# Weights' first matrix requested in another order beside the q and k of two attention groups, and one cast moved to ScalarE

## Chip, core and metric

The kernel runs on one core of one Trainium2 chip. The metric is the device time of one execution in microseconds (us); the median of seven executions is used. A profiled execution gives the trace from which all other times here are read, counted from the start of its span.

## What is computed

Causal attention in blocks of 64 over 8 batches, 8 heads, 576 positions and a head size of 64, followed by a two-branch layer over the 4608 tokens. Cut to what matters:

```python
scores = q @ k.T / 8                      # per batch and head, 576 x 576
scores = where(block_i >= block_j, scores, -1e9)
attn   = softmax(scores)
x      = (attn @ v), heads side by side   # 4608 x 512
h1, h2 = x @ w1, x @ w2                   # w1, w2: 512 x 1024
out    = maximum(h1, h2) @ w_out          # 1024 x 512
```

The kernel uses max(h1, h2) = h2 + max(h1 - h2, 0). So it needs D = w1 - w2 (`d_sb`, in bf16), M = w2 @ w_out (`m_sb`), and then out = x @ M + relu(x @ D) @ w_out.

## The kernel before, in words

**Work and tiles.** The 64 heads form 32 pairs, two pairs are a group, two groups a batch. For a group, `load_qk` fetches q and k as fp32 (0.59 MB each, issued by SP, after POOL has written one element of the target tile, which makes the request wait its turn: "gated"). `cast` makes bf16 of them, `transposes` turns them on TensorE into PSUM tiles that DVE or ScalarE copy to `qT` and `kT`. Scores (L376, and L394 with padded keys `kz`) go to PSUM, ScalarE takes exp of them into `aT` (L400), POOL zeroes the masked corners (L405), `av` multiplies with v (L491) and DVE normalises (L497, L498). `x_out` or a transposing DMA puts the result into `xT`. v is fetched by POOL in five chunks for a batch (`load_v(b, c)`), cast to bf16 on the way; the last chunk has 64 rows.

**The layer's work is filler.** `plan` lists units in a fixed order: `bT_unit` (transposes of w2), `m_unit(i, c)` (eight matmuls, one quarter of a half of M; the result is copied from PSUM to `m_sb` at L254), `h_unit(i, f)` (four matmuls with columns f of D; DVE's relu at L231 makes `g`), `y_unit`. `fill(n)` at places in the code issues the next units of the list worth n. Block j of `d_sb` (256 columns, made by `diff_w(j)` on DVE at L183 from `w1raw` and w2) is used by `h_unit(i, 2j)` and `h_unit(i, 2j + 1)`.

**The order is written out by hand.** The scheduler is off: each engine runs its instructions in the order in which the code issues them, and waits where one needs something that is not there. There are queues of this kind on PE, DVE, ScalarE (ACT), POOL and SP. POOL's queue holds casts, masks and the issue of the loads of v, w1, w2 and w_out (L159, L177, L180, L189); SP's holds the loads of q and k (L115) and the stores. Up to group 3 the order is in straight code (from L584), later a loop from L691 does one group per turn.

**Buffers.** `ps_m` has four PSUM buffers that m_units, h_units, transposes and av take in turn, so a matmul waits until the buffer's last user has been copied out. q and k have three fp32 buffers each, w1 has four, one for a block.

**The stretch at hand.** The filler ahead of group 2's q transposes is m(0,3), m(1,0) and m(1,1); m(1,2) follows q's transposes, m(1,3) k's; then come the first scores of pair 4, h_unit(0,0) and h_unit(0,1), the rest of pair 4's scores, h(0,2) and h(0,3), group 3's q transposes, h(0,4), group 3's k transposes, h(0,5), and with pair 6 the loop, whose first `av` is that of pair 4 with batch 1's v.

Of the kernel before, what the change touches and what calls it, by code (L numbers as in the profile page):

```python
# [14 lines left out]
def kernel(  # L15
# [18 lines left out]
    d_ff = moe_w1.shape[1]  # L34
# [9 lines left out]
    RPP = S // NP  # L44
# [53 lines left out]
    m_sb = wpool.tile([P, NDM, d_model], BF16, name="m_sb")  # L98
# [6 lines left out]
    dve, pool, act = nc.vector.tensor_copy, nc.gpsimd.tensor_copy, nc.scalar.copy  # L105

    def load_qk(g, queues, gated=False):
        b, u = divmod(g, GPB)
        for nm, src, queue in (("q", q, queues[0]), ("k", k, queues[1])):
            if queue is None or by_dma(nm, g):  # L110
                continue
            raws[nm, g] = t = raw.tile([P, 2, RPP * D], FP32, name=f"{nm}raw")
            if gated:
                nc.gpsimd.memset(t[:, 0, :1], 0.0)
            queue.dma_start(  # L115
                out=t[:],
                in_=src[b, 4 * u:4 * u + 4].rearrange(
                    "(s h) (p t) d -> (h p) s (t d)", h=2, t=RPP),
            )
# [4 lines left out]
    def by_dma(nm, g):  # L124
        return g >= T_DMA.get(nm, NG)
# [21 lines left out]
    def cast(nm, g, parts):  # L147
        if by_dma(nm, g):
            return
        t = raws[nm, g].rearrange("p s (t d) -> p t s d", d=D)  # L150
        if (nm, g) not in qk_n:
            qk_n[nm, g] = qkn.tile([P, RPP, 2, D], BF16, name=f"{nm}n")
        n = qk_n[nm, g]
        for copy, j0, j1 in parts:
            copy(out=n[:, j0:j1], in_=t[:, j0:j1])  # L155

    def load_v(b, c):
        rows = min(P, S - c * P)
        nc.gpsimd.dma_start(  # L159
            out=vv_r[b % NV][P - rows:, c, :, :D],  # L160
            in_=v[b, :, c * P:c * P + rows, :].rearrange("h p d -> p h d"),
        )
# [5 lines left out]
    WB = 256  # L168
# [6 lines left out]
    def load_w1(j):  # L175
        w1_raw[j] = wraw.tile([P, NDM, WB], FP32, name="w1raw")
        nc.gpsimd.dma_start(out=w1_raw[j][:], in_=w1r[:, :, j * WB:(j + 1) * WB])  # L177
# [4 lines left out]
    def diff_w(j):  # L182
        nc.vector.tensor_sub(d_sb[:, :, j * WB:(j + 1) * WB], w1_raw[j][:], w2_sb[j])  # L183
# [8 lines left out]
    dve, pool, act = nc.vector.tensor_copy, nc.gpsimd.tensor_copy, nc.scalar.copy  # L192
    SP, ACT = nc.sync, nc.scalar
# [51 lines left out]
    def m_unit(i, c):  # L245
        ds = slice(i * WH, (i + 1) * WH)
        pt = ps_m.tile([P, WH], FP32, name="ps_M", tag="m")
        for f in range(NFF):
            nc.tensor.matmul(  # L249
                pt[:], bT_sb[:, f, c * P:(c + 1) * P], wo_sb[:, f, ds],  # L250
                start=(f == 0), stop=(f == NFF - 1),
            )
            if f == NFF - 1:
                (act if i else dve)(out=m_sb[:, c, ds], in_=pt[:])  # L254
            yield

    def y_terms(i, s):
# [69 lines left out]
    def fill(n):  # L327
        while n > 0:
            if not current:
                k = next((k for k, t in enumerate(todo) if t[2] <= done_tokens[0]), None)  # L330
                if k is None:
                    return max(0, n)
                current.append(todo.pop(k))
            t = current[0]
            next(t[1])
            n -= t[3]
            t[0] -= 1
            if not t[0]:
                current.pop()
        return 0  # L340
# [10 lines left out]
    def transposes(nm, g, copies):  # L351
        n = qk_n.pop((nm, g))
        pts = [ps_m.tile([P, RPP, NP], BF16, name=f"ps_{nm}T", tag="m") for _ in range(2)]
        for j in range(RPP):
            for i in range(2):
                r = slice(i * NP, (i + 1) * NP)
                nc.tensor.transpose(  # L357
                    pts[i][:, j, :], n[r, j].rearrange("p s d -> p (s d)"), ident[r, r],
                )

        def copy_out(which=(0, 1), part=(0, NP), copy=None):
            p0, p1 = part
            for i in which:
                t = (qT_r if nm == "q" else kT_r)[(2 * g + i) % NT]
                (copy or copies[i])(  # L365
                    out=t[:, p0 * RPP:p1 * RPP].rearrange("q (p j) -> q p j", j=RPP),
                    in_=pts[i][:, :, p0:p1].rearrange("q j p -> q p j"),
                )
        return copy_out

    def scores(p, ps, col, c, q0, w):
        qT, kT = qT_r[p % NT], kT_r[p % NT]
        k0 = min(c * P, S - P)
        for hh in range(2):
            r = slice(hh * D, (hh + 1) * D)
            nc.tensor.matmul(  # L376
                ps[:, hh, col:col + w], kT[r, k0:k0 + P], qT[r, q0:q0 + w],
                start=True, stop=True,
            )


    def pad_keys(p):
        nc.gpsimd.tensor_copy(
            out=kz_r[p % NT].rearrange("p (a c) -> p a c", c=BLK)[:, 0:3:2],
            in_=kT_r[p % NT][:, S - 3 * BLK:].rearrange("p (a c) -> p a c", c=BLK)[:, 0:3:2],
        )


    def corner_scores(p, ps, col):
        qT, kz = qT_r[p % NT], kz_r[p % NT]  # L390
        for k0, q0 in ((0, 384), (BLK, 512)):
            for hh in range(2):
                r = slice(hh * D, (hh + 1) * D)
                nc.tensor.matmul(  # L394
                    ps[:, hh, col:col + BLK], kz[r, k0:k0 + P], qT[r, q0:q0 + BLK],
                    start=(k0 == 0), stop=(k0 > 0),
                )

    def exp(p, ps, w, a0):
        nc.scalar.activation(  # L400
            out=aT_r[p % NA][:, :, a0:a0 + w], in_=ps[:, :, :w], func=AF.Exp, scale=scale,
        )

    def mask(p, a0, eng=None):
        (eng or nc.gpsimd).memset(aT_r[p % NA][BLK:, :, a0:a0 + BLK], 0.0)  # L405
# [23 lines left out]
    def masks_p(p, eng=None):  # L429
        for a in (0, 256):  # L430
            mask(p, a, eng)

    def masks_q(p, eng=None):
        for a in (1024, 1408):
            mask(p, a, eng)
# [3 lines left out]
    def tile_0(p):  # L439
        u = ps_s.tile([P, 2, 512], FP32, name="ps_s", tag="s")  # L440
        scores(p, u, 0, 0, 0, 512)
        return lambda masked: (exp(p, u, 512, 0), masked and mask(p, 0))

    def tile_1(p):
        u = ps_s.tile([P, 2, 512], FP32, name="ps_s", tag="s")
        scores(p, u, 0, 0, 512, 64)
        scores(p, u, 64, 1, 128, 448)
        return lambda masked: (exp(p, u, 512, 512), masked and mask(p, 576))

    def tile_2(p):  # L450
        u = ps_s.tile([P, 2, 512], FP32, name="ps_s", tag="s")
        corner_scores(p, u, 320)
        scores(p, u, 0, 2, 256, 320)
        scores(p, u, 384, 3, 448, P)

        def out(masked):
            exp(p, u, 512, 1024)
            nc.scalar.activation(
                out=aT_r[p % NA][BLK:, :, 1536:AW], in_=u[BLK:, :, 320:320 + BLK],
                func=AF.Exp, scale=scale,  # L460
            )
            if masked:
                mask(p, 1024)
                mask(p, 1344)
        return out

    def masks(p):
        for a0 in (0, 576, 1024, 1344):
            mask(p, a0)

    def region(*tiles, masked=True):
        for out in tiles:
            out(masked)
# [146 lines left out]
    burst_p(3, 1)  # L620
    masks_p(2)
    masks_p(3)
    load_w1(0)
    fill(2)
    av(1, [2, 3, 4])
    burst_q1(2)
# [4 lines left out]
    burst_q3(2)  # L631
    masks_q(2)
    load_qk(2, (SP, SP), gated=True)
    load_w1(1)
    load_w1(2)
    fill(2)
    burst_q1(3)
    fill(2)
# [2 lines left out]
    av(2, [2, 3, 4])  # L641
    burst_q3(3)
    masks_q(3)
    load_w1(3)
    load_v(1, 0)
    load_v(1, 1)
    load_qk(3, (SP, SP), gated=True)
    fill(8)
    av(3, [2, 3, 4])
    fill(4)  # L650
    x_out(1, 0, NCH, (act, act))
    cast("q", 2, ((pool, 0, RPP),))
    cast("k", 2, ((pool, 0, RPP),))
    load_v(1, 2)
    fill(4)
    diff_w(0)
    diff_w(1)
    fill(8)
    transposes("q", 2, (dve, act))()
    diff_w(2)  # L660
    fill(4)
    transposes("k", 2, (act, act))()
    pad_keys(4)
    pad_keys(5)
    diff_w(3)
    cast("q", 3, ((pool, 0, RPP),))
    load_v(1, 3)
    load_qk(4, (SP, SP), gated=True)
    cast("k", 3, ((pool, 0, RPP),))
# [1 line left out]
    fill(4)  # L671
    region(tile_0(4), tile_1(4), masked=False)
    fill(8)
    region(tile_2(4), tile_0(5), masked=False)
    masks(4)
    fill(8)
    copy_out = transposes("q", 3, (dve, act))
    outs = tile_1(5), tile_2(5)
    copy_out()
# [96 lines left out]
```

## Time and profile before

| | us |
|---|---|
| median of 7 executions | 261.57 (261.13 to 262.75) |
| the profiled execution, its own time | 260.73 |
| its span, first to last instruction | 259.0 |
| PE busy | 242.6 |
| DVE, ACT, POOL busy | 149.1, 120.4, 122.9 |

The mean granted TensorE clock of the span was 0.993. Rows of a timeline give the start, the duration, the engine, the line and the operation. A group of waits reads "who, line, waited for <- whom: total, times, longest". A row of the table by time gives the stretch, its length, busy time of PE, PEld (weight loads), DVE, ACT and POOL with the number of instructions, and then PE's granted clock, the DMA engines' share and GB/s. A transfer's landing is counted from the start of its issue.

### The profile page before, as it was taken

The page shows a single profiled execution, that of the slowest core. Times are in us where ns is not written, and L with a number is a line of the kernel's source. Part 1 is how long each engine was busy: PE and PEld are TensorE (multiplying, and loading weights), DVE is VectorE, ACT ScalarE, POOL GpSimd, SP SyncE. Part 2 cuts the span into 40 slices and gives each one's busy share as a digit, 9 for nine tenths or more (in the row PEclk, how much of TensorE's full clock was granted, in tenths as well). Part 3 has the DMA queues.
Part 4 walks back from the last instruction along what each step waited for, and adds up shares of the span by engine and source line. Part 5 has one row for each costly group of instructions (what it writes and reads, how often), then busy time and mean ns, then how long its engine had stood idle before and what let it go on. Part 6 is the DMA issues. An engine that isn't in the chain of part 4 may idle for free.

```text
span 259.0 us, 6717 instructions
## 1 busy us (share of the span) xinstructions
PE 242.6 (94%) x2732; PEld 133.5 (52%) x2768; DVE 149.1 (58%) x299; ACT 120.4 (46%) x160; POOL 122.9 (47%) x289
## 2 busy tenths in 40 slices
PE   8798849999999999999999999999999999999994
PEld 2466734556464655555555555555555554444443
DVE  4977564756485537653764476447644754754521
ACT  2876237784956647373646464555555400000000
POOL 2976436549778684857494658456331100000000
PEclk9999988999999999999999999999999999999999
DMA  7999999469999999999999999999952302101122
GB/s 244 210 162 233 370 296 182 80 180 195 143 203 163 176 174 196 219 176 212 172 215 144 223 171 201 152 205 179 130 101 84 86 31 75 66 19 65 56 105 83
DMA packets 104383, 41.27 MB, mean 159 GB/s; under 512 B 89248, under 2 KB 93728, under 8 KB 104352
## 3 DMA queue, kind: packets, MB, share of 16 engines
q0 software_dynamic: 65952, 11.87, 59.5%
q1 hardware_dynamic: 37984, 28.32, 47.8%
q10 hardware_dynamic: 416, 0.66, 0.8%
q8 instruction: 21, 0.34, 0.6%
q14 instruction: 10, 0.08, 0.1%
HBM read 34.60 MB, written 9.44 MB: 170 GB/s over the span
## 4 chain that ended last, share of the span: by engine, by line
PE 88%; DMA 5%; ACT 2%; issue 2%; DVE 1%; POOL 1%; SPq 0%; POOLq 0%
PE ps_y L268 35%; PE ps_h L226 24%; PE ps_o L491 11%; PE ps_s L376 9%; DMA kraw<-in_k_dram 5%; PE ps_w L346 2%; PE ps_qT L357 2%; ACT aT L400 1%; PE ps_y L283 1%; PE ps_s L394 1%; PE ps_M L249 1%; PE ps_s L411 1%; PE ps_kT L357 1%; POOL kn L155 0%; PE ps_bT L238 0%
## 5 line engine op out<-in xcount | busy, mean ns | idle before, releaser
L400 ACT ACTIVATE aT<-ps_s 128x1024 bf16<-128x1024 f32 (+2 forms) x100 | 95.8, 994 | 44.4 <-PE ps_s L376 32.8
L268 PE MATMUL ps_y<-wo_sb,g 128*128 128x512 bf16 x261 | 66.7, 379 | 2.6 <-issue 2.5
L226 PE MATMUL ps_h<-xT,d_sb 128*128 128x512 bf16 x277 | 67.2, 380 | 1.2 <-issue 0.6
L231 DVE TENSOR_SCALAR g<-ps_h 128x512 bf16<-128x512 f32 x72 | 49.7, 690 | 21.3 <-PE ps_h L226 21.3
L405 POOL MEMSET aT<- 64x128 bf16 x128 | 22.9, 201 | 62.4 <-ACT aT L400 60.9
L273 DVE COPY y<-ps_y 128x512 f32<-128x512 f32 x35 | 24.2, 692 | 46.2 <-PE ps_y L268 45.6
L491 PEld LDWEIGHTS <-aT 128*128 128x128 bf16 x960 | 37.5, 98 | 14.1 <-issue 0.7
L226 PEld LDWEIGHTS <-d_sb 128*128 128x128 bf16 x288 | 26.4, 98 | 31.5 <-issue 3.6
L268 PEld LDWEIGHTS <-g 128*128 128x128 bf16 x280 | 24.7, 98 | 30.2 <-issue 5.5
L491 PE MATMUL ps_o<-vv,aT 128*128 128x65 bf16 x960 | 39.9, 194 | 0.0
L268 PE MATMUL ps_y<-m_sb,xT 128*128 128x512 bf16 x136 | 37.2, 379 | 0.4 <-PE ps_s L376 0.2
L159 POOL DMA_DIRECT2D vv<-in_v_dram x40 | 34.0, 854 | 0.9 <-issue 0.5
L376 PE MATMUL ps_s<-qT,kT 64*128 64x128 bf16 (+6 forms) x344 | 31.8, 283 | 1.4 <-ACT kT L365 0.7
L498 DVE TENSOR_TENSOR xp<-ps_o,rec 128x256 bf16<-128x256 f32 (+1 forms) x64 | 31.4, 491 | 2.2
L132 POOL DMA_DIRECT2D kb<-in_k_dram x40 | 29.4, 758 | 0.0
L497 DVE RECIPROCAL rec<-ps_o 128x4 f32<-128x4 f32 (+1 forms) x64 | 12.0, 187 | 24.2 <-PE ps_o L491 23.6
L288 ACT COPY y<-ps_y 128x256 f32<-128x256 f32 (+1 forms) x2 | 0.6, 320 | 49.3 <-PE ps_y L283 49.3
L365 ACT COPY qT<-ps_qT 128x576 bf16<-128x576 bf16 x15 | 9.6, 640 | 24.4 <-PE ps_qT L357 23.0
L155 POOL CAST qn<-qraw 128x1152 bf16<-128x1152 f32 (+1 forms) x15 | 17.0, 1135 | 7.9 <-DMA qraw<-in_q_dram 7.9
L268 PEld LDWEIGHTS <-xT 128*128 128x128 bf16 x140 | 12.8, 98 | 14.0 <-issue 0.7
L376 PEld LDWEIGHTS <-kT 64*128 64x128 bf16 x344 | 11.9, 95 | 12.6 <-issue 7.8
L365 DVE COPY qT<-ps_qT 128x576 bf16<-128x576 bf16 x17 | 12.7, 749 | 0.5 <-PE ps_qT L357 0.5
(58 smaller groups left out, 137.1 us busy)
## 6 DMA issues: line engine op xcount, KB each, us to landing
qraw<-in_q_dram SPq DMA_DIRECT2D x16, 576.0 KB, 5.2
out_dram<-y SPq DMA_DIRECT2D x35, 256.0 KB, 4.0
vv<-in_v_dram POOLq DMA_DIRECT2D x32, 128.0 KB, 5.9
kraw<-in_k_dram SPq DMA_DIRECT2D x5, 576.0 KB, 7.6
kb<-in_k_dram POOLq DMA_DIRECT2D x40, 72.0 KB, 6.8
w1raw<-in_moe_w_dram POOLq DMA_DIRECT2D x4, 512.0 KB, 11.5
xT<-in_moe_w_dram POOLq DMA_DIRECT2D x4, 256.0 KB, 6.9
wo_sb<-in_moe_w_out_dram POOLq DMA_DIRECT2D x2, 512.0 KB, 10.4
```

The lines of the kernel that those rows point to most:

```text
L132: nc.gpsimd.dma_start(out=n[h * BLK:(h + 1) * BLK, :, s], in_=(q if nm == "q" else k)[b, 4 * u + 2 * s + h].rearrange("(j p) d -> p j d", ...
L159: nc.gpsimd.dma_start(out=vv_r[b % NV][P - rows:, c, :, :D], in_=v[b, :, c * P:c * P + rows, :].rearrange("h p d -> p h d"),)
L226: nc.tensor.matmul(pt[:], d_sb[:, c, f * P:(f + 1) * P], xT[:, c, t0:t0 + SPAN], start=(c == 0), stop=(c == NDM - 1),)
L231: nc.vector.tensor_scalar_max(g[:, f], pt[:], 0.0)
L268: nc.tensor.matmul(py[:], lhs, rhs, start=(n == 0), stop=(n == len(terms) - 1),)
L273: nc.vector.tensor_copy(out=y[:], in_=py[:])
L365: (copy or copies[i])(out=t[:, p0 * RPP:p1 * RPP].rearrange("q (p j) -> q p j", j=RPP), in_=pts[i][:, :, p0:p1].rearrange("q j p -> q p j"),)
L376: nc.tensor.matmul(ps[:, hh, col:col + w], kT[r, k0:k0 + P], qT[r, q0:q0 + w], start=True, stop=True,)
L400: nc.scalar.activation(out=aT_r[p % NA][:, :, a0:a0 + w], in_=ps[:, :, :w], func=AF.Exp, scale=scale,)
L405: (eng or nc.gpsimd).memset(aT_r[p % NA][BLK:, :, a0:a0 + BLK], 0.0)
L491: nc.tensor.matmul(po[:, gi, hh, :], a[:, hh, a0:a0 + P], vv[:, c, h0 + 2 * hh, :], start=(mm == 0), stop=(mm == n_mm - 1),)
L498: nc.vector.tensor_mul(xp[:, :, ts[0]:ts[0] + n, p % 2].rearrange("q s t d -> q t s d"), po[:, :, :, :D], rec[:, :n].to_broadcast([P, n, 2 ...
```

## The change

It moves requests and steps in the hand-written order, from POOL's and DVE's queues above all. In words:

- `load_w1(0)` goes behind the masks of pair 3; `load_w1(1)` to `(3)` go behind the cast of group 2's q, which goes forward.
- Group 3's q is requested ahead of that cast, its k behind it.
- Batch 1's v chunks 0 and 1 follow the blocks of w1; chunk 2 is issued after the cast of group 3's q, beside chunk 3.
- Group 2's k is cast by ScalarE instead of POOL, behind `x_out(1)`.
- `diff_w(1)` to `(3)` move back, to behind k's transposes and between the h_units.
- The PSUM copies of m(1,0) and m(1,1) go from ScalarE to DVE.

```diff
-                (act if i else dve)(out=m_sb[:, c, ds], in_=pt[:])
+                (act if i and c > 1 else dve)(out=m_sb[:, c, ds], in_=pt[:])
...
     masks_p(3)
-    load_w1(0)
     fill(2)
...
     load_qk(2, (SP, SP), gated=True)
-    load_w1(1)
-    load_w1(2)
     fill(2)
...
     masks_q(3)
-    load_w1(3)
+    load_w1(0)
+    load_qk(3, (SP, None), gated=True)
+    cast("q", 2, ((pool, 0, RPP),))
+    load_qk(3, (None, SP), gated=True)
+    for j in range(1, d_ff // WB):
+        load_w1(j)
     load_v(1, 0)
     load_v(1, 1)
-    load_qk(3, (SP, SP), gated=True)
     fill(8)
     av(3, [2, 3, 4])
     fill(4)
     x_out(1, 0, NCH, (act, act))
-    cast("q", 2, ((pool, 0, RPP),))
-    cast("k", 2, ((pool, 0, RPP),))
-    load_v(1, 2)
+    cast("k", 2, ((act, 0, RPP),))
     fill(4)
     diff_w(0)
-    diff_w(1)
     fill(8)
     transposes("q", 2, (dve, act))()
-    diff_w(2)
     fill(4)
     transposes("k", 2, (act, act))()
     pad_keys(4)
     pad_keys(5)
-    diff_w(3)
+    diff_w(1)
     cast("q", 3, ((pool, 0, RPP),))
+    load_v(1, 2)
     load_v(1, 3)
     load_qk(4, (SP, SP), gated=True)
     cast("k", 3, ((pool, 0, RPP),))
...
     region(tile_0(4), tile_1(4), masked=False)
     fill(8)
+    diff_w(2)
     region(tile_2(4), tile_0(5), masked=False)
     masks(4)
     fill(8)
+    diff_w(3)
     copy_out = transposes("q", 3, (dve, act))
```

## Prediction

> **What bounds the kernel now.** I read the page first, then the chain of waits in order of time, then PE's waits, then the rows of the transfers, then the table by microsecond. Times without a unit are microseconds (us) from the span's start.
>
> ```profile
> PE 242.6 (94%) x2732; PEld 133.5 (52%) x2768; DVE 149.1 (58%) x299; ACT 120.4 (46%) x160; POOL 122.9 (47%) x289
> PE 88%; DMA 5%; ACT 2%; issue 2%; DVE 1%; POOL 1%; SPq 0%; POOLq 0%
> ```
>
> TensorE is busy 94% of the span and is 88% of the chain that ended last. Only one other thing has weight: DMA with 5%, and the chain in order of time shows that this is a single piece.
>
> ```profile
> 22.23 13.25 DMA kraw<-in_k_dram
> 35.60 1.16 POOL kn L155
> 36.81 0.47 PE ps_kT L357 x18
> 37.28 1.82 PE ps_M L249 x8
> 39.09 0.97 PE ps_s L376 x6
> 40.06 0.33 issue
> 40.39 1.73 PE ps_h L226 x7
> ```
>
> Group 2's k is asked for at 22.23 and lands 13.25 later; POOL casts it, and only then can PE transpose it. PE's own waits, and its clock just after, give the price:
>
> ```profile
> PE ps_kT L357 <- POOL kn L155: 3.3, 1, 3.3
> PE ps_qT L357 <- POOL qn L155: 1.0, 1, 1.0
> ...
> 37.00:38.00 1.00, 1.00 (x22) 0.70 (x15) 0.98 (x1) 0.69 (x2) 0.58 (x1) 0.54 1.91 217
> 38.00:39.00 1.00, 1.00 (x6) 0.45 (x3) 0.00 (x0) 0.48 (x1) 0.75 (x3) 0.50 1.70 136
> 39.00:40.00 1.00, 1.00 (x7) 0.30 (x7) 0.00 (x0) 0.62 (x2) 1.00 (x2) 0.50 1.65 105
> 40.00:41.00 1.00, 0.67 (x5) 0.47 (x5) 0.00 (x0) 1.00 (x2) 1.00 (x4) 0.75 0.39 31
> ```
>
> PE loses 3.3 for k and 1.0 for q. After the 3.3 its granted clock (third number from the end) is about a half until 40.5: eight matmuls of L249 take 1.82, where eight took 0.87 earlier; six of scores take 0.97 instead of 0.61. That is 1.4 more, so some 5.7 lie in this place. Everything behind it is PE work, back to back, so what is won here and not given back shows in the total.
>
> **Why k is late: the bytes in front of it.**
>
> ```profile
> L177 POOL DMA_DIRECT2D w1raw<-in_moe_w_dram x4: 751/754/767, 18.4 to 24.4; - x4
> DMA to landing us min/median/max: 10.1/11.5/12.3
> ...
> 23.00:24.00 1.00, 0.52 (x13) 0.30 (x9) 0.87 (x3) 1.00 (x2) 0.63 (x2) 1.00 1.46 194
> 24.00:25.00 1.00, 0.58 (x6) 0.53 (x7) 0.16 (x1) 0.05 (x1) 0.85 (x2) 1.00 1.40 264
> 25.00:26.00 1.00, 1.00 (x12) 0.90 (x10) 0.42 (x1) 0.00 (x0) 1.00 (x3) 1.00 1.10 381
> ```
>
> The last column is GB/s. Up to about 24.8 the small pieces of w_out hold it at 200; then it runs at 340 to 390 until 37. I take 0.36 MB/us. The blocks of w1 (0.52 MB each) land at 29.8, 32.0, 34.3 and 36.65; q and k of group 2 (0.59 MB each) at 30.2 and 35.5; of group 3 at 37.25 and 39.0. They take turns: 3.87 MB from 24.8 to q3 make 10.7, which is 35.6, so a landing comes some 1 to 1.6 after that sum.
>
> **The change, part by part.** *Moved requests.* SP still asks for q2 and k2 at 21.8 and 22.2. In front of k2 now lie only q2 and w1's block 0 (issued by POOL at 24.35, behind two memsets): 1.70 MB, 4.7, so 29.5 and with the lag 30.7 (35.5 before). For q2, with its own bytes and some of block 0, 27.7 and the lag: 29.2. For block 0 the nearest rows give two ends: one block in turns takes 2.3 (the distance of the landings) after w_out's last landing at 27.5, so 29.8; behind all that is asked for earlier (q2, k2, q3: 2.29 MB in all) 31.2 to 31.6. I take 30.6, the middle. *DMA: Bandwidth & Descriptors* of the Trainium skill, section "Anatomy of one DMA", gives a transfer 2.0 us plus bytes over 436 GB/s: 3.2 for a block, which would land at 27.6 and cost PE nothing. The rows say 10.1 to 12.3 for a block in company, so I stay with the bytes in front; by the page the sum below would be 0.8 better at its first step.
>
> *PE up to the first h_unit.* m(1,1) ends at 31.09 as before. q's cast (1.15, on POOL) ends at 30.4, or 30.9 if it meets DVE's subtraction as before (it took 1.65 then): q's wait of 1.0 is gone, transposes to 31.5. New is that DVE has diff_w(0) in front of the PSUM copies of m(1,0) and m(1,1), which ScalarE did: 30.6 + 1.23 + 0.42 = 32.3 before m(1,2) gets its buffer. That is a new PE wait of 0.8. m(1,2) to 33.15. k's cast on ScalarE: 640 elements took 0.725 at the start, 1152 by ScalarE's about 1.04 ns each 1.27; 30.7 + 1.27 = 32.0, and q's copy queued behind it (0.64) ends at 32.65, under m(1,2). k's transposes 33.15 to 33.5, m(1,3) to 34.4 with kT's copy under it, scores to 35.0. So h_unit(0,0) starts at 35.0 instead of 40.39: 5.4 won.
>
> *DVE behind it.* The subtractions now stand between the relus and, the last, in front of qT's copy of group 3. Block 1 is issued at about 30.5 and shares with k3: (0.52 + 0.59)/0.36 from 32.2 is 35.3. diff_w(1) ends near 36.7. Then DVE has until group 3's k copy, which the scores of pair 6 need: five relus of 0.69, two subtractions of 1.23, two copies of 0.75: 7.4, less 0.6 since DVE's rows start about 0.07 before the one ahead has ended: 43.5. Those scores began at 47.85, so of 5.4 there are 4.2 left. Blocks 2 and 3 (1.05 MB more: 38.2) are there in time.
>
> *POOL's queue.* POOL now waits for q2 with q3's memset behind it done, but with k3's memset (it gates SP's request), three blocks of w1 (0.75 each), v(1,0) and v(1,1) (0.89 each), the key pads, q3's cast, v(1,2), v(1,3), q4 and k4's memsets, k3's cast and v(1,4) queued. From 30.4 that gives: k3 30.5, blocks to 32.8, v(1,1) 34.6, q3's cast 36.7, v(1,3) 38.4, q4 38.5, v(1,4) to 40.4. SP's order is the same, its waits are for those memsets. k3 and q4 are asked for 3.0 later and 2.4 earlier than before, v(1,0) 7.7 later, v(1,4) 1.6 earlier.
>
> *What is late next.* av of pair 4 needs v(1,4). Before, it was issued at 41.9, landed 7.1 later at 49.0 and was used at 50.69. The bytes after 24.8 are the same as before. After: 2.29 MB to 31.2, a hole to 32.2 until k3 and block 1 arrive, k3 and three blocks 2.16 MB to 38.2, four v of 0.131 MB at 0.105 MB/us (the row 39 to 40, where v ran alone) 5.0, q4 and k4 3.3, v(1,4) 0.6: 47.1, landing about 47.4; with q2 a microsecond later, and a hole as long as that of before (31 and 28 GB/s from 40 to 42), 49.3. I take 48.0. PE would be there at 50.69 - 4.2 = 46.5; only the last of its 24 matmuls need that chunk, so av ends at 48.3 instead of 51.4. **3.1 are left.** Here the same page speaks against the change, in "Issuing engines are not separate DMA queues": all queues run on the same 16 engines and interleave. If order bought nothing, v(1,4) would land at 49.0 again and the gain be 1.9. The landings above show that order counts for q2 and k2, yet for the last piece of a fixed sum of bytes the rule is nearly right, so I go halfway.
>
> *Costed at nothing:* POOL's k cast that falls away (1.15, off the path); two PSUM copies of 0.42 on DVE, counted above; the clock: gaps of 0.8 and about 1.1 are like the 0.97 at 31.1, after which the clock stayed at 1.00.
>
> The sum is against the profiled execution: 260.73 with a span of 259.0. That is 0.84 under the median of the seven, 261.57. So 257.6 there, 258.5 in the median.
>
> **The rivals.** (a) *v on time.* If v's pieces go ahead of q4 and k4, v(1,4) lands before 46.5: 4.2, 257.4. For: q4's first bytes came only as v(1,3) ended, at 42.5. (b) *Bytes decide.* v(1,4) at 49.3: av ends at 49.6, 1.8 won, 259.8. (c) *k2 doesn't land earlier*, its queue being slow by itself (5.3 behind q2): k's wait stays, within 0.5 of 261.5. Against: k4 came 1.7 behind q4 with no w1 beside it. (d) *Slower: block 0 late.* DVE is in order, and while diff_w(0) waits, the PSUM copies behind it hold PE. h_unit(0,0) starts at block 0's landing + 1.23 + 0.42 + 0.87 + 0.37 + 0.87 + 0.61, so + 4.4; from a landing at 36.0 it is later than 40.39. The block issued at this very moment before landed at 36.65. Then it starts at 41.05, and the idle stretch from 31.5 to 38.3 halves the clock again, 1.4: 2.1 lost, 263.7. Against: three blocks that lay in front of that one are gone.
>
> **How the numbers follow.** A measurement of this kernel can tell about 0.3%, 0.8 us, from no change. The forecast (2.3 to 4.0 won) gets 0.42, (a) 0.25, (b) 0.17, (c) 0.08, (d) 0.08. Faster takes the first three and no more, 0.84; same 0.07 from (c); slower (d) and the rest of (c), 0.09. The range reaches from 256.9, (a) with DVE half a microsecond shorter, to 261.2, at the near edge of (c); (d) and most of (c) are outside.
>
> **What would show it.** k2 landing near 31 and PE's wait for kn gone; no half clock near 37 to 40; PE waiting at L249 for DVE by 0.8; h_unit(0,0) near 35; scores of pair 6 near 43.6; a PE wait at L491 for vv of 1 to 2 near 47. If block 0 lands after 33, if k2 is not there by 32, or if PE has no wait for vv, a step is wrong.

## The result, and the profile after

| | before | after |
|---|---|---|
| median | 261.80 (260.45 to 263.42, 31 runs) | 258.45 (257.82 to 260.96, 12 runs) |
| the profiled execution, its own time | 260.73 | 258.35 |
| its span | 259.0 | 256.5 |
| mean granted clock of its span | 0.993 | 1.000 |

The ratio of after to before is 0.9884, with a 95% interval of 0.9863 to 0.9905. The medians lie 3.35 us apart, the two profiled executions 2.4. The prediction had 258.5 for the median and 257.6 for a profiled execution.

The page of the kernel after, busy times and the chain that ended last:

```profile
PE 240.4 (94%) x2732; PEld 133.1 (52%) x2768; DVE 150.6 (59%) x301; ACT 120.5 (47%) x159; POOL 121.1 (47%) x288
PE 83%; DMA 7%; DVE 4%; issue 3%; ACT 2%; POOL 0%; POOLq 0%
```

TensorE is busy for 2.2 less; most of that is the half clock of before, which is gone (some 1.4 by the prediction's rows). DVE's share of the chain has gone from 1% to 4%. The chain in order of time (start, duration, what) shows where:

```profile
21.59 6.73 DMA qraw<-in_q_dram
...
29.56 6.30 DMA w1raw<-in_moe_w_dram
...
35.88 1.90 DVE d_sb L183
37.78 0.24 issue
38.02 1.27 DVE g L231 x2
39.29 0.90 DVE d_sb L183
40.19 0.76 issue
40.95 1.27 DVE g L231 x2
42.22 1.13 DVE d_sb L183
43.35 0.67 DVE qT L365
44.02 0.60 DVE g L231
44.62 0.68 DVE kT L365
45.30 0.05 issue
45.34 0.61 PE ps_s L376 x6
```

Group 2's k is no longer in the chain. It was asked for at 22.00 and landed 9.5 later, at 31.5. In its place stands w1's block 1 (landed 35.86), and from there to the scores of pair 6 all is DVE: three subtractions, relus and copies, one after the other. PE's waits after ("who, line, waited for <- whom: total, times, longest"):

```profile
PE ps_M L249 <- DVE m_sb L254: 1.6, 1, 1.6
...
PE ps_h L226 <- DVE qT L365: 1.0, 1, 1.0
...
PE ps_h L226 <- DVE g L231: 0.7, 1, 0.7
```

The waits for `kn` (3.3) and `qn` (1.0) are gone; there is none for `vv`. The new ones are all for DVE. In the table by time the third number from the end is the granted clock, about a half from 37.1 to 40.5 before:

```profile
38.00:39.00 1.00, 1.00 (x10) 0.41 (x5) 1.00 (x3) 0.83 (x1) 1.00 (x4) 1.00 2.41 178
...
41.00:42.00 1.00, 0.34 (x2) 0.29 (x3) 1.00 (x3) 1.00 (x2) 0.23 (x2) 1.00 1.79 159
43.00:44.00 1.00, 0.07 (x6) 0.09 (x1) 1.00 (x3) 0.94 (x3) 0.00 (x0) 1.00 1.29 275
```

The clock is full. In the last two rows PE (first busy share) mostly stands idle, while DVE (third) has no gap. The transfers of w1's blocks, of which the three that went out around q and k before had landed 10.1 to 12.3 after their issue:

```profile
L177 POOL DMA_DIRECT2D w1raw<-in_moe_w_dram x4: 751/754/767, 24.1 to 31.0; - x4
DMA to landing us min/median/max: 6.3/7.1/8.2
```

DVE's subtractions, by the timeline of its queue:

```profile
31.34 1.23 DVE L183 TENSOR_TENSOR d_sb<-w1raw,xT 128x1024 bf16<-128x1024 f32 x1 [1.68 <-DMA w1raw<-in_moe_w_dram]
35.88 2.21 DVE L183 TENSOR_TENSOR d_sb<-w1raw,xT 128x1024 bf16<-128x1024 f32 x1 [1.99 <-DMA w1raw<-in_moe_w_dram]
39.21 1.81 DVE L183 TENSOR_TENSOR d_sb<-w1raw,xT 128x1024 bf16<-128x1024 f32 x1
42.14 1.21 DVE L183 TENSOR_TENSOR d_sb<-w1raw,xT 128x1024 bf16<-128x1024 f32 x1
```

and POOL's casts of group 3's q and k:

```profile
35.87 1.15 POOL L155 CAST qn<-qraw 128x1152 bf16<-128x1152 f32 x1
38.77 1.16 POOL L155 CAST kn<-kraw 128x1152 bf16<-128x1152 f32 x1
```

All four subtractions have the same size. The two that begin while a cast is running, at 35.88 and 39.21, take 2.21 and 1.81, the others 1.23 and 1.21. The casts keep their 1.15. If a subtraction makes no progress until the cast is over, it ends at 35.87 + 1.15 + 1.21 = 38.23 and 38.77 + 1.16 + 1.21 = 41.14; the rows end at 38.09 and 41.02.

One number serves for every kernel below: the time from the start of group 4's q transposes (the first PE work behind the av of pair 4) to the end of the span. It is 259.0 - 51.34 = 207.7 before and 256.5 - 48.84 = 207.7 after. In the traces of the experiments it lies between 207.6 and 207.9. So the total is decided by when PE gets to that point.

### The profile page after: what moved, and what is told of

The parts are those of the page before. It is cut to its first block, busy times and chain, and to the rows that moved or that the text cites. A ratio compares the mean times of both kernels' runs of the same rounds, so it can differ in the third digit from the quotient of the medians.

```text
span 256.5 us, 6716 instructions
## 1 busy us (share of the span) xinstructions
PE 240.4 (94%) x2732; PEld 133.1 (52%) x2768; DVE 150.6 (59%) x301; ACT 120.5 (47%) x159; POOL 121.1 (47%) x288
## 4 chain that ended last, share of the span: by engine, by line
PE 83%; DMA 7%; DVE 4%; issue 3%; ACT 2%; POOL 0%; POOLq 0%
PE ps_y L268 35%; PE ps_h L226 23%; PE ps_o L491 11%; PE ps_s L376 8%; DMA qraw<-in_q_dram 5%; DMA w1raw<-in_moe_w_dram 2%; PE ps_qT L357 2%; DVE d_sb L183 2%; ACT aT L400 2%; DVE g L231 1%; PE ps_y L283 1%; PE ps_s L394 1%; PE ps_s L411 1%; PE ps_kT L357 0%; PE ps_bT L238 0%
## 5 line engine op out<-in xcount | busy, mean ns | idle before, releaser
L491 PEld LDWEIGHTS <-aT 128*128 128x128 bf16 x960 | 37.5, 98 | 14.1 <-issue 0.7
L491 PE MATMUL ps_o<-vv,aT 128*128 128x65 bf16 x960 | 39.9, 194 | 0.0
L288 ACT COPY y<-ps_y 128x256 f32<-128x256 f32 (+1 forms) x2 | 0.6, 319 | 49.3 <-PE ps_y L283 49.3
L376 PEld LDWEIGHTS <-kT 64*128 64x128 bf16 x344 | 11.9, 94 | 12.3 <-issue 7.1
```

What stands on the lines that cost most here:

```text
L376: nc.tensor.matmul(ps[:, hh, col:col + w], kT[r, k0:k0 + P], qT[r, q0:q0 + w], start=True, stop=True,)
L491: nc.tensor.matmul(po[:, gi, hh, :], a[:, hh, a0:a0 + P], vv[:, c, h0 + 2 * hh, :], start=(mm == 0), stop=(mm == n_mm - 1),)
```

## The experiments

Each was timed in five rounds against the kernel before on the same chip; the ratio stands with its 95% interval. The first four ran on one chip, `e5`, `e6`, `e7` and `e9` on a second, the last three on a third.

### The new cast on ScalarE: back to POOL

```diff
-    cast("k", 2, ((act, 0, RPP),))
+    cast("k", 2, ((pool, 0, RPP),))
```

> The changed kernel, but group 2's k is cast by POOL again, at the same place in the code, which is behind POOL's issue of v(1,1) (ended at 33.57). So the cast is at about 33.6 to 34.8 and k's transposes start near 34.8 instead of 33.92. Theory A (from block 1's landing on, DVE's queue sets the time: the subtraction of block 1 began at 35.88 whatever PE did): the scores of pair 6 stay near 45.3, total within 0.4 us of the changed kernel's 258.45. Theory B (PE's own path to the first h_unit counts in full): 0.8 us later there and at the end, 259.3.

Measured: 259.51, ratio 0.9924 (0.9894 to 0.9954), span 257.4. PE's waits:

```profile
PE ps_M L249 <- DVE m_sb L254: 2.1, 1, 2.1
PE ps_o L491 <- DMA vv<-in_v_dram: 1.1, 1, 1.1
```

POOL cast k at 33.09 in 1.18, and no PE wait for `kn` came back: k was ready at 34.27, just before PE wanted it at 34.38, since PE stood at m(1,2) for longer. The scores of pair 6 even began earlier (44.85 against 45.34): block 1 landed 0.5 earlier, and its subtraction took 1.23, for no cast was running when it began. But v(1,4) was issued at 41.48 instead of 39.86 and landed at 49.3 instead of 47.4, and now av waits for it.

The extra cast is not what pushed POOL's queue. POOL stood idle for 1.28 behind it, waiting for `kT`; then this row came (the copies of the key pads):

```profile
35.55 1.49 POOL L383 COPY kz<-kT 128x128 bf16<-128x128 bf16 x2 [1.28 <-ACT kT L365]
```

One of the two copies took 1.25, where each takes 0.3 in the changed kernel's profile. It ran beside block 1's subtraction, which had begun first, at 35.42. A later profile of the changed kernel itself (`e12_changed_again`) shows the same without the extra cast: a pad copy of 1.32, v(1,4) issued at 40.91 and landed at 48.54, span 257.5, ratio 0.9920. The run with the cast on POOL, at 257.4 and 0.9924, is not told apart from it. So what the cast on ScalarE is worth is not shown.

### The subtractions back at their old places

```diff
     diff_w(0)
+    diff_w(1)
...
     transposes("q", 2, (dve, act))()
+    diff_w(2)
...
-    diff_w(1)
+    diff_w(3)
```

(`diff_w(2)` and `diff_w(3)` are taken out between the h_units.)

> The changed kernel with its requests as they are, but diff_w(1) to (3) at the places that they had before the change, so that diff_w(1) stands in front of the PSUM copies of m(1,0) and m(1,1). Theory A (DVE in order, held by a block that isn't there): block 1 lands near 35.9, m(1,2) can't start before about 37.5 instead of 32.95, PE stands idle for some 6 us, its clock halves again, h_unit(0,0) starts at 41 to 42.5, total 262 to 264, not faster than the kernel before. Theory B (the gain is in the order of the requests alone, the places of the subtractions are by the way): within 1 us of 258.45.

Measured: 263.31, ratio 1.0055 (1.0036 to 1.0074), slower than before. PE's waits:

```profile
PE ps_M L249 <- DVE m_sb L254: 6.2, 1, 6.2
```

The blocks land as in the changed kernel; block 1 is there at 36.0. But DVE is in order and `diff_w(1)` stands in front of the PSUM copies that free m(1,2)'s buffer. PE idles 6.2 and then runs at half clock, m(1,2) taking 1.86. h_unit(0,0) starts at 42.15, later than the 40.39 of before. k of group 2 landed at 31.0, so its early landing comes with the moved requests and not with the places of the subtractions. The moved requests and the moved subtractions belong together: without the second the rest of the change costs 0.55% instead of winning 1.2%.

### Block 0's subtraction behind q's transposes

```diff
-    diff_w(0)
     fill(8)
     transposes("q", 2, (dve, act))()
+    diff_w(0)
```

> The changed kernel with diff_w(0) behind q's transposes of group 2, so that the PSUM copies of m(1,0), m(1,1) and q's copy don't wait for block 0. PE's wait of 1.64 for DVE at m(1,2) should go; k's transposes then wait for k's cast and q's copy on ScalarE (33.3), so h_unit(0,0) starts 0.6 earlier, at 35.4. Theory A (block 1's landing at 35.86 sets DVE, DVE sets the scores of pair 6): those stay near 45.3 and the total within 0.3 of 258.45. Theory B (the PE wait is worth its row): 0.6 to 1.6 us faster.

Measured: 257.25 (256.91 to 257.53), ratio 0.9819 (0.9796 to 0.9842), span 255.7. h_unit(0,0) starts at 35.02, the place of the prediction's own sum, and the wait of 1.6 at L249 is gone. DVE's timeline:

```profile
31.80 1.22 DVE L183 TENSOR_TENSOR d_sb<-w1raw,xT 128x1024 bf16<-128x1024 f32 x1
35.97 1.23 DVE L183 TENSOR_TENSOR d_sb<-w1raw,xT 128x1024 bf16<-128x1024 f32 x1 [2.95 <-DMA w1raw<-in_moe_w_dram]
38.31 1.70 DVE L183 TENSOR_TENSOR d_sb<-w1raw,xT 128x1024 bf16<-128x1024 f32 x1
41.13 1.21 DVE L183 TENSOR_TENSOR d_sb<-w1raw,xT 128x1024 bf16<-128x1024 f32 x1
```

Block 1 landed no earlier, and yet the scores of pair 6 came at 44.33 instead of 45.34. The reason is the second row: with PE ahead, the key pads and behind them q's cast on POOL came earlier (34.84 to 35.99), so the subtraction met no cast and took 1.23. The theory that block 1's landing would hold everything at its place falls; it held the start of the subtraction, not its end.

### Block 3's subtraction later

```diff
-    diff_w(3)
...
     transposes("k", 3, (dve, act))()
+    diff_w(3)
```

> The changed kernel with diff_w(3) behind group 3's k transposes, so that q's copy, one relu and k's copy of group 3 go ahead of it on DVE. Theory A (DVE's queue sets the scores of pair 6): they start near 44.2 instead of 45.34, h_unit(0,6) waits for the subtraction until about 45.5 (45.88 in the changed kernel), total 0.4 to 1.0 us faster. Theory C (v(1,4), which landed at 47.4, is the next bound at once): PE gets a wait for vv at L491 and at most 0.6 us are won.

Measured: 258.43 (257.59 to 260.44), ratio 0.9871 (0.9838 to 0.9905): not told apart from the changed kernel. In the profile the piece from h_unit(0,0) to the scores of pair 6 was 45.55 - 37.89 = 7.66, against 9.31 in the changed kernel, and h(0,6) then waits 0.5 for `d_sb`. Not all of that is the edit: PE came late here, and block 1's subtraction was over (35.65, 1.23) before h_unit(0,0) began. The nearest comparison is the later profile of the changed kernel, `e12_changed_again`, where PE was late too and that subtraction took 1.22: 46.41 - 37.37 = 9.04. But the execution of `e4` had a half clock after its wait at m(1,2), from PE's timeline:

```profile
33.25 1.83 PE L249 MATMUL ps_M<-wo_sb,bT_sb 128*128 128x256 bf16 x8 [2.15 <-DVE m_sb L254]
```

where the same eight took 1.03 behind a wait of 1.64 in the changed kernel. That swallows what was won, so as a total this run is inconclusive.

### The cast of group 3's k away from the subtractions

On top of `e3_sub0_late`:

```diff
     load_qk(4, (SP, SP), gated=True)
-    cast("k", 3, ((pool, 0, RPP),))
     load_v(1, 4)
...
     masks(4)
+    cast("k", 3, ((pool, 0, RPP),))
```

> The kernel with diff_w(0) behind q's transposes (257.25 us), and group 3's k cast by POOL behind the masks of pair 4 instead of ahead of v(1,4). Theory L (DVE's subtraction and a POOL cast that has begun exclude each other: subtractions that began just behind a cast took 1.7 to 2.2, others 1.23): the subtraction of block 2 takes 1.23 instead of 1.70, the scores of pair 6 start near 43.9 instead of 44.33, total 0.3 to 0.6 us faster. Theory M (the longer subtractions come from the transfers into SBUF in those microseconds, not from the casts): block 2's stays near 1.7 and the total the same.

Measured: 257.06, ratio 0.9832 (0.9802 to 0.9862), span 255.8. The casts of POOL's timeline stand at 35.67 and 40.02; DVE's:

```profile
36.76 1.23 DVE L183 TENSOR_TENSOR d_sb<-w1raw,xT 128x1024 bf16<-128x1024 f32 x1 [2.03 <-DMA w1raw<-in_moe_w_dram]
39.10 1.22 DVE L183 TENSOR_TENSOR d_sb<-w1raw,xT 128x1024 bf16<-128x1024 f32 x1
41.44 1.22 DVE L183 TENSOR_TENSOR d_sb<-w1raw,xT 128x1024 bf16<-128x1024 f32 x1
```

No subtraction begins more than 0.06 before the end of a cast, and none is longer than 1.23; the rival, that transfers into SBUF in those microseconds make them longer, expected 1.7 for block 2. This shows the collision, edited away at one place. From h_unit(0,0) to the scores of pair 6 it is 8.80, instead of 9.31 in `e3_sub0_late`. The total is that of `e3_sub0_late` within the accuracy; in this execution the whole stretch had begun 0.8 later, behind a wait for w_out.

### Both subtractions later, and v asked for earlier

`e6_sub0_sub3_late` joins the edits of `e3_sub0_late` and `e4_sub3_late`. `e7_v_ahead` adds to it:

```diff
     load_v(1, 1)
+    load_v(1, 2)
+    load_v(1, 3)
+    load_v(1, 4)
```

(the three are taken out at their later places).

> The kernel with diff_w(0) behind q's transposes (257.25 us), and diff_w(3) behind group 3's k transposes too. The scores of pair 6 should start near 43.0 to 43.3 instead of 44.33. Theory C (v(1,4), issued at 38.8 and landing at 47.7, is then the bound): PE waits 1 us or more for vv at L491 near 46.5, the total is within 0.3 of 257.25. Theory A (DVE's queue was the only bound here): no such wait, 0.8 to 1.2 us faster.

> The kernel with diff_w(0) and diff_w(3) late, and v(1,2), v(1,3), v(1,4) issued by POOL right behind v(1,1), ahead of the key pads, so ahead of the requests of q4 and k4. Theory C (v(1,4)'s place in the queue is the bound once DVE's queue is shorter): v(1,4) lands before 46, PE's wait for vv is gone, total 0.7 to 1.3 us below the same kernel with v at its old place, near 256.2. Rival D (the sum of bytes is the same, so q4 comes late instead): POOL waits for q4, PE waits at group 4's q transposes by 1 us or more, nothing won.

Measured: 256.86, ratio 0.9820 (0.9791 to 0.9850), span 255.5; and 256.70, ratio 0.9815 (0.9785 to 0.9845), span 255.6. With both edits PE is at the scores of pair 6 at 42.79, 2.5 earlier than in the changed kernel, but only 1.1 of that reaches group 4's transposes (47.76). Of the rest, 0.5 is a wait of h(0,6) for the subtraction that was moved back. PE's timeline of the first shows the next bound:

```profile
46.05 0.44 PE L491 MATMUL ps_o<-vv,aT 128*128 128x65 bf16 x9
47.18 0.64 PE L491 MATMUL ps_o<-vv,aT 128*128 128x65 bf16 x15 [0.69 <-DMA vv<-in_v_dram]
```

v(1,4) landed at 47.4 and av waits for it. Asking for v earlier does not help: in the second kernel v(1,4) was issued at 34.9 and took

```profile
DMA to landing us min/median/max: 8.6/9.1/12.3
```

12.3, to 47.2. So the place in POOL's queue does not decide there. q and k of group 4 were asked for 2.4 and 2.9 behind it and landed before it, at 45.4 and 47.0: the bytes in flight beside it are the likely cause, but they were not varied alone. PE lost on the other side what it had waited for v: with the issues of v in front, the pad copies and q's cast on POOL came later, and block 1's subtraction, begun while such a copy ran and with the cast right behind it, took 2.51.

### A second block beside q and k

On top of `e3_sub0_late`:

```diff
     load_w1(0)
+    load_w1(1)
     load_qk(3, (SP, None), gated=True)
```

> The kernel with diff_w(0) behind q's transposes (257.25 us), with block 1 of w1 issued right behind block 0, ahead of group 2's q cast: the part of the change that holds back a second block is undone. k2 (landed at 31.1) should come 0.7 to 1.4 later, block 1 (35.9) 2 earlier. Theory A (block 1's landing sets DVE, DVE sets the scores of pair 6): the subtraction of block 1 is done before the first relu, the scores of pair 6 don't move or come earlier, total the same or up to 0.8 faster. Theory B (the bytes in front of k2 are what counts): PE waits for k's cast by about 1 us more and the total rises by 0.7 to 1.4.

Measured: 257.21, ratio 0.9840 (0.9810 to 0.9872), span 254.9. k of group 2 landed at 29.3, no later than in the changed kernel, and block 1 at 33.3 instead of 35.9. ScalarE's timeline:

```profile
29.44 1.15 ACT L155 CAST kn<-kraw 128x1152 bf16<-128x1152 f32 x1 [0.82 <-DMA kraw<-in_k_dram]
```

Before, blocks 1 and 2 went out from 21.93 on, at the same moment as q's and k's requests; blocks 0 and 1 here go out from 24.35 on, 2 behind them, and k doesn't suffer. The moment of the request may count, not only the bytes; it was not varied alone. And k's landing scatters: with one block behind it, it lay between 29.8 and 31.5 in nine traces (30.8 and 31.5 for the changed kernel itself); with two, at 29.3, 30.5 and 30.6 (`e9`, `e11`, `e10`). Holding back block 1, as the change does, was not needed for k. The time won at block 1 was spent on other waits (1.3 for DVE, 0.6 for k's cast, 0.6 for v), and the total stays where it was.

### k of group 4 behind v

`e11_k4_behind_v` adds to `e9_block1_first`:

```diff
-    load_qk(4, (SP, SP), gated=True)
+    load_qk(4, (SP, None), gated=True)
     cast("k", 3, ((pool, 0, RPP),))
     load_v(1, 4)
...
     masks(4)
+    load_qk(4, (None, SP), gated=True)
```

`e10_k4_behind_v_sub3_late` has block 3's subtraction late as well, and `e12_changed_again` is the changed kernel itself, on the same chip.

> The kernel with block 1 right behind block 0 and diff_w(0) behind q's transposes (257.21 us), with the request of group 4's k split from its q and put behind the masks of pair 4, so behind v(1,4). Theory E (v(1,4), which landed at 47.0 to 47.9 wherever its issue stood, is bound by the bytes in front of it, those of k4 among them): v(1,4) lands 1.2 to 1.6 earlier, near 45.6, PE's wait for vv of 0.6 goes, group 4's q transposes start at 46.4 to 46.8 instead of 47.31, total 0.5 to 0.9 us faster; PE doesn't wait for k4, which it needs 4 us later. Rival D (what v wins k4 loses): PE waits for kn at k4's transposes and the total stays.

> As the kernel with k4's request behind v(1,4), and diff_w(3) behind group 3's k transposes. Theory E: with DVE's queue shorter (scores of pair 6 near 41.5 instead of 43.1) and v(1,4) near 45.6, PE reaches av of pair 4 near 44.7, waits about 1 us for vv, group 4's q transposes start near 46, total 255.3 to 256.0. Rival D: v lands at 47 as ever, PE waits 2 us or more for it, total 257.

> The changed kernel itself, on the same chip as the two others, for a comparison with them. All theories: 258.2 to 258.7 us; group 4's q transposes near 48.8, no PE wait for vv, subtractions of 1.7 to 2.2 where a POOL cast began just before them.

Measured: 256.27 (256.08 to 256.86), ratio 0.9805 (0.9772 to 0.9838); 256.41, ratio 0.9810 (0.9779 to 0.9840); and the changed kernel 259.26 (258.70 to 259.71), ratio 0.9920 (0.9891 to 0.9948). In the first, v(1,4) was issued at 41.80, nearly two later than in the changed kernel, and landed earlier, at 46.4, with k of group 4 (0.59 MB) asked for behind it. av does not wait. The second has the same order of requests, and there v(1,4) landed at 47.0, as in `e9_block1_first`, and av waits 0.3. So it is not shown that moving k brings v earlier. PE's waits in this stretch are now for casts:

```profile
PE ps_kT L357 <- POOL kn L155: 1.4, 1, 1.4
PE ps_qT L357 <- POOL qn L155: 0.4, 1, 0.4
```

This version beats both kernels: 3.0 less than the changed kernel on the same chip (256.27 against 259.26). Against `e3_sub0_late` the intervals overlap, so how much of it comes from the last two edits is not settled. `e10` moves one subtraction more and gains nothing: a wait for `d_sb` of 0.5 comes, and waits of 0.3 for v and 1.2 for the casts.

The repeat of the changed kernel lies above the 258.2 to 258.7 that were expected, and its profile differs from the one of the result in two places. The first is who pays in the collision. DVE's row for block 1 and POOL's for a pad copy:

```profile
35.61 1.22 DVE L183 TENSOR_TENSOR d_sb<-w1raw,xT 128x1024 bf16<-128x1024 f32 x1 [1.68 <-DMA w1raw<-in_moe_w_dram]
35.66 1.32 POOL L383 COPY kz<-kT 128x128 bf16<-128x128 bf16 x1 [0.25 <-ACT kT L365]
```

Block 1 landed 0.3 earlier, so the subtraction began just ahead of POOL's copy instead of behind it; now the copy is the longer one. The second is the clock, by the table by time for the stretch behind the wait at m(1,2):

```profile
34.00:35.00 1.00, 1.00 (x23) 0.77 (x23) 0.00 (x0) 0.94 (x3) 0.00 (x0) 0.76 1.03 373
35.00:36.00 1.00, 1.00 (x7) 0.45 (x5) 0.39 (x1) 0.60 (x2) 0.63 (x2) 0.50 1.05 356
36.00:37.00 1.00, 1.00 (x7) 0.32 (x8) 0.83 (x1) 0.67 (x2) 1.00 (x2) 0.50 1.00 344
37.00:38.00 1.00, 0.67 (x4) 0.39 (x4) 0.00 (x0) 1.00 (x2) 1.00 (x1) 0.54 1.53 247
```

A half clock of 3.4 in all, some 1.7 lost (an estimate: half of it). The wait ahead of it was 2.2 here and in `e4`; it was 1.6 in the profile of the result and 2.1 in that of `e1`, and there the clock stayed at 1.00. The section "What's actually happening" of the Trainium skill's page *TensorE: Matmul & The Clock Gate* has the clock set by activity in a free-running window of 3.4; with such a window the same wait can fall in it well or badly. No run here shows the window itself, but the runs fit it: the mean granted clock of the changed kernel was between 0.985 and 1.000 in the 18 runs. In all kernels that have no wait at m(1,2) (`e3`, `e5`, `e6`, `e7`, `e9`, `e10`, `e11`) it was 0.997 or more in each of 34 runs.

## Why the prediction was right, and where it was not

**The landings.** k of group 2 was put at 30.7, q at 29.2, block 0 at 30.6; they came at 31.5, 28.3 and 31.3. The bytes in front gave this within 0.9. For k that is in part luck: by the same sum a second block (0.52 MB, 1.4) would have put it at 32.1, and it came at 29.3 to 30.6 in the three traces that have one (`e9`, `e11`, `e10`). By the prediction's estimate from *DMA: Bandwidth & Descriptors* of the Trainium skill, section "Anatomy of one DMA", block 0 would have taken 3.2; it took 7.2.

**PE up to the first h_unit.** The wait for DVE came as said, at L249, but 1.64 long instead of 0.8: block 0 was 0.7 late, and that is nearly all of it. h_unit(0,0) started at 36.03 instead of 35.0, so 4.4 were won instead of 5.4. The half clock of before went, as said. Left unsaid was that the new wait could bring it back: the trace had 0.97 as the only short wait and the prediction took that as a sign that shorter ones are free. At 1.6 to 2.2 they sometimes are and sometimes are not.

**DVE behind it: the step that failed.** The prediction let block 1's subtraction end at 36.7 and counted "two subtractions of 1.23" behind it, to have the scores of pair 6 at 43.5. They came at 45.34. Block 1 landed at 35.86 instead of 35.3, 0.6. Its subtraction then took 2.21 instead of 1.23, and block 2's 1.81: 1.0 and 0.6, both behind a cast on POOL that the change itself had brought there (group 3's q and k are cast while DVE now subtracts). The trace of before had shown the other side of this: q's cast began 0.58 behind a subtraction there and took 1.65. The prediction took that as a property of the cast, and gave the subtraction none. The page *SBUF — State Buffer* of the Trainium skill, section "Who interferes with whom", says that a DVE instruction with two inputs in SBUF and a GpSimd instruction that reads SBUF block each other, and that the order of issue decides which one waits. The rows agree: 1.65 for the cast where the subtraction was first, 2.21 and 1.81 for the subtractions where the cast was first, and 1.23 at most for all of them in `e5`.

**v.** v(1,4) landed at 47.4, which is the prediction's sum of the bytes; it had gone to 48.0 for fear of a hole. But PE did not wait: the loss on DVE brought it to av only at 48.02. The step "PE wait at L491 for vv of 1 to 2" is therefore wrong for the changed kernel, and right as a bound that stood just behind. It appears as soon as POOL is later (`e1`, 1.1) or PE earlier (`e6`, 0.7; `e9`, 0.6). The page *DMA: Bandwidth & Descriptors*, section "Issuing engines are not separate DMA queues", has the DMAs of all issuing engines interleave on the same DMA engines; from that the prediction took that order might buy nothing, and went halfway. For this last piece the runs are nearer to "nothing": an issue 3.3 earlier, from `e6` to `e7`, moved the landing by 0.2. With k of group 4 behind v it came at 46.4 and 47.0 (`e11`, `e10`), against 47.0 in `e9`.

**The total.** The chain won 2.5 (group 4's transposes at 48.84 instead of 51.34), not 3.1, and the profiled execution 2.4. So of the forecast, 0.6 was given away on DVE. The median fell by 3.35 all the same; on the third chip, with the changed kernel again, it fell by 2.5 (261.76 to 259.26). The profiled execution of before was one with a single half-clock stretch, 0.993. Of the 39 later runs of the kernel before that ran beside the experiments, the ten at 0.992 or 0.993 have a median of 260.85 and the 29 below that, nearly all at 0.986 or 0.987, one of 262.10. That is about the size of a second half-clock stretch; where it would lie is not shown. Of the twelve runs of the kernel after, eight have 0.998 or more, so no half-clock stretch. So the sum against the profile was 0.7 too good, and the median of before lies higher above its profiled execution than the prediction knew (1.1 instead of 0.84, against 0.1 after). That the number met the median so closely is in this part luck.

**The rivals.** (a), v on time, is nearest to what happened to v, but its 4.2 did not come, for DVE took it. (b) and (c) did not occur. (d), the slower one, had block 0 late for its cause; the block came at 31.3, so it did not decide. Its mechanism is real: `e2` brings it about by the order of DVE's queue alone and loses 0.55%, some 1.4, where 2.1 was the price.

**What stays open.** Why three subtractions were long with no cast or copy on POOL when they began: 2.08 and 1.72 in `e1`, 1.78 in `e6`. POOL was issuing DMA requests then, but it did so beside others that took 1.23 (`e9`, at 36.60). Which of the moved requests freed k of group 2: of them only block 1 was put back (`e9`), and k did not suffer. And which waits between 1.6 and 2.2 halve the clock: 1.8 did not in `e7`, 2.1 did not in `e1`, 2.2 did in `e4` and `e12`, and no run here varied the wait alone.

## What to carry to other kernels

When a change moves work of one engine beside that of another, price it by the rows that ran beside such work, not by the row's lone duration: a subtraction of 1.23 was one of 2.21 beside a cast. In an in-order queue, an instruction that waits for a transfer goes behind everything that frees a buffer for the bounding engine; moving one such line (`e3`) was worth over 1 us more. And after each win look for the next bound just behind: here k, then DVE's copies, then the collision, then v. Last, profile the same kernel twice before explaining a difference of a microsecond: here two profiles of the changed kernel, on two chips, lie 1.0 apart.

## What the runs showed that was not expected

- A subtraction of fp32 and bf16 (128x1024) on DVE and a cast (128x1152) on POOL don't run side by side: 1.23 becomes 1.70 to 2.21 behind a cast (`e3`, after), 1.15 becomes 1.65 behind a subtraction (before). A small copy in SBUF on POOL is caught too: 0.3 becomes 1.25 and 1.32 (`e1`, `e12`).
- Which of the two waits can change from one execution of the same kernel to another (here on another chip): block 1's subtraction took 2.21 in one profile of the changed kernel and 1.22 in the other, where POOL's copy took the wait.
- The last chunk of v, 64 KB, landed at 47.2, 47.4, 46.4 and 47.0 when issued at 34.9, 38.2, 41.8 and 41.4 (`e7`, `e6`, `e11`, `e10`): 12.3, 9.2, 4.6 and 5.6 in flight.
- Two blocks of w1 requested some 2 us behind q and k left k at 29.3 to 30.6 (`e9`, `e11`, `e10`); with two requested at the same moment and one ahead, before, it came at 35.5.
- A wait of 2.2 on PE, behind back-to-back work, was followed by 3.4 of half clock in two profiles (`e4`, `e12`); one of 2.1 was not (`e1`).
